# A decode step with gated attention and MLP: the result's cast and write, SP's last wait, and the place of the first load

## The chip, the cores and the metric

The kernel runs on one core of a Trainium2 chip. The core has five engines with instruction queues of their own: TensorE (PE, with its weight loads shown apart as PEld), VectorE (DVE), ScalarE (ACT), GpSimd (POOL) and SyncE (SP, which here only issues DMAs and waits). Sixteen DMA engines move data between the chip's memory (HBM) and the on-chip memory (SBUF); matmuls write to PSUM, in banks of 512 fp32 columns. Engines meet only through semaphores. The metric is the device time of one execution in microseconds.

## The reference

One decode step for four sequences (B = 4) with one new position each. Attention reads the last 4096 positions of a key and value cache with 8 key heads and 32 query heads of 128; an MLP with a ReLU gate runs on the same input; a scalar gate per sequence mixes the two. B_x is not used.

```
g = sigmoid((x * gate_w).sum(-1))              # one number per sequence
q = (x @ wq) -> 32 heads of 128                # x: 4 x 512
p = softmax(q @ k^T / sqrt(128))               # last 4096 of 16384 positions
a = (p @ v) -> 4 x 4096, then @ wo             # 4 x 512
b = ((x @ W_gate) * (x @ W_gate > 0) * (x @ W_up)) @ W_down
out = g * a + (1 - g) * b                      # 4 x 512, bf16
```

All inputs are bf16. The kernel reads 81 MB and writes 4 KB.

## The kernel before

The program is written as a list of operations per engine (class Program, lines 34 to 150). `op` and `dma` append an operation with a name and the names it waits for; `plan` turns these into semaphore values, leaving out waits that an engine has already made; `emit` (line 107) writes an engine's list out. PE's list is written as a loop over pairs of sets; the other engines' lists are straight. All five lists are written out inside one block (lines 562 to 581): at its start each engine jumps to its own code, and at its end each engine drains and all meet in a barrier. A barrier of all engines also stands at the start of the program, under line 595, ahead of the block.

All large loads are issued by SP, in the order in which they are needed (lines 245 to 261): wq (4 MB), then for each of eight sets (a sequence and half of its key heads) K and V of 4 MB each, with two buffers of each, then W_gate, W_up, W_down and wo in four pieces of 2, 1.25, 0.5 and 0.25 MB. A load into a buffer waits for the last reader of what was there. x (4 rows of 1 KB) and gate_w (1 KB) are issued by ACT (lines 243 and 244).

At the start x and gate_w are transposed on PE (line 306), the gate g and 1 - g are made (lines 311 to 319, event G), and q is projected (line 457) when wq has landed. For each set the keys are transposed on PE (line 340) and copied back by ACT and DVE (lines 345, 347), the scores are made (line 373), masked (line 381) and exponentiated (line 410), turned (line 417) and multiplied with V (line 429); `combine` (line 437) adds the parts and writes the attention output, scaled by g and by the softmax sum, into the tile `oq` (line 450). The MLP's hidden values, scaled by 1 - g, go into `hT` (line 483).

Both tiles serve as weights of the last matmuls, with 32 columns for each contraction slice of 128. Only four columns, one for each sequence, hold values, and the rest stay zero. Before the change sequence b stands in column 8b. The last matmuls (lines 545 and 553) are four column tiles side by side: tile c writes rows 32c to 32c + 31 of one bank, with output columns 128c to 128c + 127, so that sequence b's result stands in row 32c + 8b. They accumulate over W_down and then over the pieces of wo as those land.

The end (lines 557 to 559):

```
P.op("dve", lambda e: e.tensor_copy(outs[:, :], AB[:, 0:128]), ("OUTS",), [("ACC",)])
P.dma("sp", ... out.rearrange("b o (c d) -> c (b o) d", d=128), outs[0:128:8, :]), ("OUT",), [("OUTS",)])
P.op("sp", None, None, [("OUT",)])
```

DVE casts the whole bank, 128 rows of 128 columns, to bf16; SP writes every eighth row to its place in the result, sixteen pieces of 256 B; then SP waits for that write, still inside the block, so that the barrier at the block's end comes behind it.

Of the kernel before, what the change touches and what calls it, by code (L numbers as in the profile page):

```python
# [6 lines left out]
BF16 = mybir.dt.bfloat16  # L7
ACTF = mybir.ActivationFunctionType
# [25 lines left out]
class Program:  # L34
# [69 lines left out]
            if name is not None:  # L104
                ins.then_inc(sems[self.events[name][0]], step)

    def emit(self, engine, eng, sems):
        ops, plan = self.ops[engine], self.plan(engine)
        if engine != "pe":
            for op, need in zip(ops, plan):  # L110
                self.put(eng, sems, op, need)
            return
        n = len(self.turns) - 1
        base = []
        for t in range(n + 1):
            level = {}
            for need in plan[:self.turns[t]]:
                level.update({s: v for s, v in need.items() if s in self.lowered})
            base.append(level)
        shift = [{s: base[t + 1].get(s, 0) - base[t].get(s, 0) for s in self.lowered} for t in range(n)]  # L120
        length = self.turns[1] - self.turns[0]
        bodies = []
        for t in range(n):
            assert shift[t] == shift[0] and self.turns[t + 1] - self.turns[t] == length
            body = []
            for k in range(length):
                need = plan[self.turns[t] + k]
                body.append({s: v - base[t].get(s, 0) for s, v in need.items() if s in self.lowered})
                if t > 0:
                    assert all(s in self.lowered for s in need), (t, k, need)  # L130
                    a, b = ops[self.turns[t] + k][1], ops[self.turns[0] + k][1]
                    assert (a is None) == (b is None) and (a is None or self.events[a][0] == self.events[b][0])
            bodies.append(body)
            assert body == bodies[0], [(k, x, y) for k, (x, y) in enumerate(zip(body, bodies[0])) if x != y]
        for k in range(self.turns[0]):
            self.put(eng, sems, ops[k], plan[k])
        for s, v in base[0].items():
            eng.sem_inc(sems[s], -v)
        with eng.Fori(0, n):
            for k in range(length):  # L140
                i = self.turns[0] + k
                need = dict(bodies[0][k])
                need.update({s: v for s, v in plan[i].items() if s not in self.lowered})
                self.put(eng, sems, ops[i], need)
            for s, v in shift[0].items():
                if v:
                    eng.sem_inc(sems[s], -v)
        for i in range(self.turns[n], len(ops)):
            self.put(eng, sems, ops[i], {s: v - base[n].get(s, 0) if s in self.lowered else v
                                         for s, v in plan[i].items()})  # L150


def bass_gated_mix__sliding_block_cached__glu_gated_reglu__decode_kernel(
# [13 lines left out]
    with ExitStack() as ctx:  # L167
        def sb(name, shape, dt):
            return ctx.enter_context(nc.sbuf_tensor(name, shape, dt))
# [33 lines left out]
        recip = sb("recip", [128, 2], FP32)  # L203
        oq = sb("oq", [128, 32, 32], BF16)
        gtmp = sb("gtmp", [128, NFT * 4], FP32)
        gtmp2 = sb("gtmp2", [128, NFT * 4], FP32)
        hT = sb("hT", [128, NFT, 32], BF16)
        outs = sb("outs", [128, 128], BF16)
        banks = [ctx.enter_context(nc.psum_tensor("bank%d" % i, [128, 512], FP32)) for i in range(8)]
        TR = banks[0:NTR]  # L210
        SCB = banks[NTR:NTR + NSC]
# [1 line left out]
        FB = banks[7]  # L213
# [7 lines left out]
        P = Program()  # L221
# [36 lines left out]
        for k in range(len(WO_CUTS) - 1):  # L258
            lo, hi = 512 * WO_CUTS[k], 512 * WO_CUTS[k + 1]
# [14 lines left out]
        for a in range(4):  # L274
            r = slice(32 * a, 32 * a + 32)
# [161 lines left out]
        def combine(s):  # L437
            par, b, half = s % 2, s // 2, s % 2
            r = slice(64 * half, 64 * half + 64)
            for k in range(8):  # L440
                lo = 3 - k % 4 + 64 * (k // 4)
                P.op("pe", lambda e, k=k, lo=lo: e.matmul(FB[r, 256:288], Wsel[:, lo:lo + 64], osb[:, par, 32 * k:32 * k + 32],  # L442
                                                          start=(k == 0), stop=(k == 7)), None,
                     [("OSB", s), ("WSUM",), ("QC", 1), ("G",), ("OQ", s - 1) if s >= 1 else None, ("H",) if s == NSET - 1 else None])
            P.op("pe", lambda e: e.matmul(FB[r, 288:288 + NPIECE], Wsum[:, :], rowsum[:, par, :], start=True, stop=True),
                 ("SUMS", s))
            P.op("dve", lambda e: e.tensor_reduce(ssum[r, par:par + 1], FB[r, 288:288 + NPIECE], AXIS.X, ALU.add),
                 ("SSUM", s), [("SUMS", s)])
            P.op("dve", lambda e: e.reciprocal(recip[r, par:par + 1], ssum[r, par:par + 1]), ("RECIP", s), [("SSUM", s)])
            P.op("dve", lambda e: e.tensor_scalar(oq[r, :, 8 * b], FB[r, 256:288], recip[r, par:par + 1],  # L450
                                                  gsb[r, b:b + 1], op0=ALU.mult, op1=ALU.mult),
                 ("OQ", s), [("RECIP", s), ("G",), ("OQZ",)])

# [18 lines left out]
        def gateup():  # L472
            for i in range(NFT):
                for which, W, key in ((0, Wg, "WG"), (1, Wu, "WU")):
                    col = 64 + 64 * which + 4 * i
                    for t in range(4):
                        P.op("pe", lambda e, W=W, i=i, t=t, col=col: e.matmul(  # L477
                            FB[:, col:col + 4], W[:, t, i:i + NFT * 127 + 1:NFT], xT[:, t * 8:t * 8 + 4],
                            start=(t == 0), stop=(t == 3)),
                            ("GU",) if (i == NFT - 1 and which == 1 and t == 3) else None, [("WG",), ("WU",), ("OQ", NSET - 2)])  # L480
            P.op("dve", lambda e: e.tensor_scalar(gtmp[:, :], FB[:, 64:64 + NFT * 4], 0.0, None, op0=ALU.max), ("H0",), [("GU",)])
            P.op("dve", lambda e: e.tensor_tensor(gtmp2[:, :], FB[:, 128:128 + NFT * 4], gtmp[:, :], ALU.mult), ("H1",), [("H0",)])
            P.op("dve", lambda e: e.tensor_tensor(
                hT[:, :, :].rearrange("p i (b o) -> p i b o", o=8)[:, :, :, 0], gtmp2[:, :].rearrange("p (i b) -> p i b", b=4),
                gsb[:, 4:8].rearrange("p (o b) -> p o b", o=1).to_broadcast([128, NFT, 4]), ALU.mult), ("H",),
                [("H1",), ("G",), ("HZ",)])

# [9 lines left out]
        for s in range(1, NSET):  # L497
# [13 lines left out]
            if s >= 2:  # L511
                combine(s - 2)
# [20 lines left out]
        for k in range(NPIECE):  # L533
            exponent(NSET - 1, k)
        combine(NSET - 2)
        for k in range(NPIECE):
            turn(NSET - 1, k)
        gateup()
        for k in range(4):
            values(NSET - 1, k)  # L540
        combine(NSET - 1)
        AB = SCB[0]
        for i in range(NFT):
# [5 lines left out]
        for k in range(len(WO_CUTS) - 1):  # L549
            for i in range(WO_CUTS[k], WO_CUTS[k + 1]):  # L550
                for cb in range(4):
# [2 lines left out]
                        AB[32 * cb:32 * cb + 32, 0:128], oq[:, i, :], Wo3[:, i, cb * 128:(cb + 1) * 128],  # L554
                        start=False, stop=(i == 31), tile_position=(0, 32 * cb)),
                        ("ACC",) if last else None, [("WO", k), ("OQ", NSET - 1)])
        P.op("dve", lambda e: e.tensor_copy(outs[:, :], AB[:, 0:128]), ("OUTS",), [("ACC",)])
        P.dma("sp", lambda e: e.dma_start(out.rearrange("b o (c d) -> c (b o) d", d=128), outs[0:128:8, :]), ("OUT",), [("OUTS",)])
        P.op("sp", None, None, [("OUT",)])

        sems = {name: ctx.enter_context(nc.semaphore(name)) for name in P.sems}
        with nc.Block() as block:
            @block.sync
            def _(e):
                P.emit("sp", e, sems)

            @block.gpsimd
            def _(e):
                P.emit("pool", e, sems)

            @block.tensor
            def _(e):
                P.emit("pe", e, sems)

            @block.vector
            def _(e):
                P.emit("dve", e, sems)

            @block.scalar
            def _(e):  # L580
                P.emit("act", e, sems)


# [26 lines left out]
```

## Time and profile before

| | |
|---|---|
| time, median of 3 runs | 197.55 us (197.55 to 197.69) |
| the profiled execution's own time | 197.38 us |
| its span, first to last instruction | 195.7 us |
| share of the span: PE, DVE, ACT | 72%, 53%, 47% |
| DMA: bytes, mean rate over the span | 81.19 MB, 415 GB/s |
| last piece of wo awaited until | 192.7 us |
| cast of the result | 193.19, 0.29 us |
| issue of the result's DMA | 193.51, 0.69 us |

A page of the profile shows one execution. A row in order of time gives the start in us, the length in us, engine, line and operation, and tile written "<-" tile read. "SPq" is SP's queue, "ACTq" ACT's. A row of groups gives the number of instructions, the busy time and the mean ns of one, and the idle time ahead of them with what ended it. A row of waits reads "who <- whom: us in total, times, longest us". A row of a window gives its limits and length, the busy time of PE, PEld, DVE, ACT and POOL with the number of instructions, and at the end PE's granted clock, the DMA engines' share and GB/s. In rows with three numbers between slashes these are the least, median and greatest duration in ns.

### The profile page before, as it was taken

Reading aid. Unit: us, or ns where it says so; the run is one execution under the profiler, and the core shown is the slowest. Engines: PE = TensorE matmul, PEld = TensorE weight load, DVE = VectorE, ACT = ScalarE, POOL = GpSimd, SP = SyncE. Lnnn points to the kernel's source line nnn. Section 1 sums busy time; section 2 is a strip of 40 time slices with the busy share of each in tenths; the row PEclk is TensorE's granted clock in tenths of the full one; section 3 lists DMA queues with packets and bytes.
Section 4 is the critical chain, followed back from the end, with each engine's and each line's share of the span. In section 5 each row is a group of like instructions: output and inputs, shape, how many; then the busy total and the mean of one; then the engine's idle time right before and its main releaser. Section 6 shows DMA issues by size and latency. Waiting matters only on the chain.

```text
span 195.7 us, 4263 instructions
## 1 busy us (share of the span) xinstructions
PE 140.6 (72%) x1858; PEld 107.7 (55%) x1858; DVE 103.6 (53%) x278; ACT 91.5 (47%) x108; POOL 7.9 (4%) x39
## 2 busy tenths in 40 slices
PE   0134199968889919992999399929992999498634
PEld 0034197535567518751976286528752875397533
DVE  2102025888599456945585659456945584741200
ACT  2000058698398409760886098509750976220000
POOL 7400000000000000000000000000000000000000
PEclk9999999999999996997599879996996699965855
DMA  6999999999999999999999999999999999999991
GB/s 215 449 429 452 429 449 442 425 429 437 432 422 429 425 429 429 427 429 425 435 429 435 429 429 430 429 429 429 429 429 429 435 411 425 450 431 415 422 385 59
DMA packets 3498, 81.19 MB, mean 415 GB/s; under 512 B 409, under 2 KB 414, under 8 KB 670
## 3 DMA queue, kind: packets, MB, share of 16 engines
q1 hardware_dynamic: 3476, 81.01, 96.8%
q8 instruction: 9, 0.15, 0.3%
q14 instruction: 3, 0.02, 0.0%
q10 hardware_dynamic: 10, 0.01, 0.0%
HBM read 81.01 MB, written 0.00 MB: 414 GB/s over the span
## 4 chain that ended last, share of the span: by engine, by line
DMA 57%; PE 25%; ACT 9%; DVE 4%; issue 1%; SPq 1%
DMA Ksb<-in_A_k_cache_dram 46%; PE bank L340 16%; DMA Wbig<-in_A_wo_dram 12%; ACT Ksb L345 7%; PE bank L373 5%; DVE Ksb L347 2%; PE bank L429 2%; ACT sc L410 2%; PE bank L553 1%; PE bank L442 1%; DVE pT L417 1%; ACT L410 1%; DVE sc L381 1%; SPq L260 0%; DVE oq L450 0%
## 5 line engine op out<-in xcount | busy, mean ns | idle before, releaser
L345 ACT ACTIVATE Ksb<-bank 128x1024 bf16<-128x1024 bf16 x72 | 70.9, 1022 | 68.2 <-PE bank L340 68.0
L340 PE MATMUL bank<-identf,Ksb 128*128 128x128 f32 x512 | 81.1, 313 | 29.4 <-DMA Ksb<-in_A_k_cache_dram 24.0
L340 PEld LDWEIGHTS bank<-identf,Ksb 128*128 128x128 f32 x512 | 66.6, 161 | 44.1 <-DMA Ksb<-in_A_k_cache_dram 25.7
L347 DVE COPY Ksb<-bank 128x1024 bf16<-128x1024 bf16 x56 | 38.0, 685 | 41.8 <-PE bank L340 40.8
L381 DVE CUSTOM_DVE_ANT_0 sc<-bank,mask 128x512 bf16<-128x512 f32 x32 | 21.7, 684 | 9.6 <-PE bank L373 9.5
L429 PE MATMUL bank<-Vsb,pT 128*32 128x256 bf16 x512 | 20.8, 291 | 0.9 <-DMA Vsb<-in_A_v_cache_dram 0.9
L373 PE MATMUL bank<-Ksb,QSP 128*32 128x512 bf16 x256 | 19.4, 383 | 2.1 <-DVE Ksb L347 1.6
L410 ACT ACTIVATE sc<-sc,negmax 128x1024 bf16<-128x1024 bf16 x16 | 18.3, 1146 | 4.8 <-DVE negmax L402 4.7
L417 DVE STREAM_TRANSPOSE pT<-sc 128x1024 bf16<-128x1024 bf16 x16 | 19.7, 1237 | 1.3 <-ACT sc L410 1.0
L429 PEld LDWEIGHTS bank<-Vsb,pT 128*32 128x32 bf16 x512 | 13.2, 101 | 7.1 <-issue 3.3
L442 PEld LDWEIGHTS bank<-osb,Wsel 128*64 128x64 f32 x128 | 8.1, 138 | 4.6 <-issue 2.6
L442 PE MATMUL bank<-osb,Wsel 128*64 128x32 f32 x128 | 8.9, 224 | 1.2 <-DVE osb L434 1.2
L373 PEld LDWEIGHTS bank<-Ksb,QSP 128*32 128x32 bf16 x256 | 4.1, 94 | 9.4 <-DVE Ksb L347 4.4
L477 PE MATMUL bank<-xT,Ksb 128*128 128x4 bf16 x112 | 6.9, 199 | 1.8 <-DVE oq L450 1.8
L477 PEld LDWEIGHTS bank<-xT,Ksb 128*128 128x128 bf16 x112 | 6.8, 160 | 1.9 <-issue 1.9
L553 PE MATMUL bank<-Wbig,oq 128*32 128x128 bf16 x128 | 4.2, 311 | 4.1 <-DMA Wbig<-in_A_wo_dram 4.0
L357 POOL COPY QSP<-QS 128x64 bf16<-128x64 bf16 x8 | 1.8, 236 | 118.2 <-PE bank L373 107.4
L457 PE MATMUL bank<-xT,Wbig 128*128 128x4 bf16 x128 | 3.6, 166 | 4.0 <-DMA Wbig<-in_A_wq_dram 4.0
L306 PE MATMUL bank<-ident,xsb 5*128 5x5 bf16 x4 | 0.3, 167 | 7.9 <-DMA xsb<-in_gate_w_dram 7.9
L553 PEld LDWEIGHTS bank<-Wbig,oq 128*32 128x32 bf16 x128 | 3.1, 140 | 5.0 <-DMA Wbig<-in_A_wo_dram 5.0
L457 PEld LDWEIGHTS bank<-xT,Wbig 128*128 128x128 bf16 x128 | 3.5, 104 | 4.0 <-DMA Wbig<-in_A_wq_dram 4.0
L434 DVE COPY osb<-bank 128x256 f32<-128x256 f32 x8 | 3.4, 420 | 3.6 <-PE bank L429 3.6
(55 smaller groups left out, 47.0 us busy)
## 6 DMA issues: line engine op xcount, KB each, us to landing
Ksb<-in_A_k_cache_dram SPq DMA_DIRECT2D x8, 4096.0 KB, 22.9
Vsb<-in_A_v_cache_dram SPq DMA_DIRECT2D x8, 4096.0 KB, 32.0
Wbig<-in_A_wq_dram SPq DMA_DIRECT2D x1, 4096.0 KB, 12.2
Wbig<-in_A_wo_dram SPq DMA_DIRECT2D x1, 2048.0 KB, 20.2
Ksb<-in_B_W_gate_dram SPq DMA_DIRECT2D x1, 1792.0 KB, 17.9
Ksb<-in_B_W_up_dram SPq DMA_DIRECT2D x1, 1792.0 KB, 21.8
Vsb<-in_B_W_down_dram SPq DMA_DIRECT2D x1, 1792.0 KB, 15.6
Wbig<-in_A_wo_dram SPq DMA_DIRECT2D x1, 1280.0 KB, 22.8
```

The source lines that it names most:

```text
L340: P.op("pe", lambda e, bk=bk, cc=cc, c=c, s=s: e.transpose(bk[:, cc * 128:(cc + 1) * 128], kw[:, c * 128:(c + 1) * 128], identf[:, :]), (" ...
L345: P.op("act", lambda e: e.activation(dst, bk[:, :].bitcast(BF16), ACTF.Copy), ("KTC", s, i), [("KT", s, i)])
L347: P.op("dve", lambda e: e.tensor_copy(dst, bk[:, :].bitcast(BF16)), ("KTC", s, i), [("KT", s, i)])
L373: P.op("pe", lambda e, a=a, h=h: e.matmul(bk[32 * a:32 * a + 32, 0:512], QSP[:, s % 2, h, :], k4[:, 16 * bank:16 * bank + 16, 32 * a:32 * ...
L381: P.op("dve", lambda e: e.tensor_tensor_reduce(sc[:, s % 2, bank * 512:(bank + 1) * 512], bk[:, :], mask[:, :], 1.0, LOWEST, ALU.add, ALU.max,
L410: P.op("act", lambda e: e.activation(sc[:, par, k * PW:(k + 1) * PW], sc[:, par, k * PW:(k + 1) * PW], ACTF.Exp, bias=negmax[:, par:par + ...
L417: P.op("dve", lambda e: e.transpose(pT[:, par, k * PW:(k + 1) * PW], sc[:, par, k * PW:(k + 1) * PW]), ("PTT", s, k), [("EXP", s, k), ("PV ...
L429: P.op("pe", lambda e, c=c, g=g, col=col: e.matmul(OB[32 * g:32 * g + 32, 0:256], pT[:, par, col:col + 32], v3[:, 16 * k + c, :], start=(k ...
L442: P.op("pe", lambda e, k=k, lo=lo: e.matmul(FB[r, 256:288], Wsel[:, lo:lo + 64], osb[:, par, 32 * k:32 * k + 32], start=(k == 0), stop=(k ...
L457: P.op("pe", lambda e, h=h, t=t: e.matmul(FB[:, 64 + 4 * h:68 + 4 * h], Wq3[:, t, 128 * h:128 * h + 128], xT[:, t * 8:t * 8 + 4], start=(t ...
L477: P.op("pe", lambda e, W=W, i=i, t=t, col=col: e.matmul(FB[:, col:col + 4], W[:, t, i:i + NFT * 127 + 1:NFT], xT[:, t * 8:t * 8 + 4], star ...
L553: P.op("pe", lambda e, i=i, cb=cb: e.matmul(AB[32 * cb:32 * cb + 32, 0:128], oq[:, i, :], Wo3[:, i, cb * 128:(cb + 1) * 128], start=False, ...
```

## The change

It has four parts.

1. The four live columns of `oq` and `hT` are columns 0 to 3 instead of 0, 8, 16 and 24. So the result stands in rows 32c to 32c + 3 of the bank.
2. The result tile `outs` is 4 rows of 512 columns instead of 128 rows of 128. Four casts of 4 rows by 128 columns fill it, c = 0 and 2 on DVE, 1 and 3 on ACT; each shifts its rows to rows 0 to 3. SP's write waits for both engines and is a plain copy of four rows of 1 KB.
3. SP's last operation, the wait for that write, is written out behind the block, so behind the block's barrier.
4. SP's first operation, the load of wq, is written out ahead of the block, behind the start-up barrier.

```diff
-    def emit(self, engine, eng, sems):
+    def emit(self, engine, eng, sems, lo=0, hi=None):
         ops, plan = self.ops[engine], self.plan(engine)
         if engine != "pe":
-            for op, need in zip(ops, plan):
+            for op, need in list(zip(ops, plan))[lo:hi]:
                 self.put(eng, sems, op, need)
...
-        outs = sb("outs", [128, 128], BF16)
+        outs = sb("outs", [4, 512], BF16)
...
-            P.op("dve", lambda e: e.tensor_scalar(oq[r, :, 8 * b], FB[r, 256:288], recip[r, par:par + 1],
+            P.op("dve", lambda e: e.tensor_scalar(oq[r, :, b], FB[r, 256:288], recip[r, par:par + 1],
...
-                hT[:, :, :].rearrange("p i (b o) -> p i b o", o=8)[:, :, :, 0], gtmp2[:, :].rearrange("p (i b) -> p i b", b=4),
+                hT[:, :, 0:4], gtmp2[:, :].rearrange("p (i b) -> p i b", b=4),
...
-        P.op("dve", lambda e: e.tensor_copy(outs[:, :], AB[:, 0:128]), ("OUTS",), [("ACC",)])
-        P.dma("sp", lambda e: e.dma_start(out.rearrange("b o (c d) -> c (b o) d", d=128), outs[0:128:8, :]), ("OUT",), [("OUTS",)])
+        for c in range(4):
+            to, src = outs[0:4, 128 * c:128 * c + 128], AB[32 * c:32 * c + 4, 0:128]
+            if c % 2 == 0:
+                P.op("dve", lambda e, to=to, src=src: e.tensor_copy(to, src), ("OUTS", c), [("ACC",)])
+            else:
+                P.op("act", lambda e, to=to, src=src: e.activation(to, src, ACTF.Copy), ("OUTS", c), [("ACC",)])
+        P.dma("sp", lambda e: e.dma_start(out.rearrange("b o d -> (b o) d"), outs[:, :]), ("OUT",), [("OUTS", c) for c in range(4)])
         P.op("sp", None, None, [("OUT",)])
...
+        P.emit("sp", nc.sync, sems, 0, 1)
         with nc.Block() as block:
             @block.sync
             def _(e):
-                P.emit("sp", e, sems)
+                P.emit("sp", e, sems, 1, -1)
...
+        P.emit("sp", nc.sync, sems, -1)
```

## The prediction

> **What bounds the kernel now.** I read the page's slices first, then a summed window, then the tail and the head in order of time, and last the waits of SP's queue and the rows of the block's end.
>
> ```profile
> span 195.7 us, 4263 instructions
> PE 140.6 (72%) x1858; PEld 107.7 (55%) x1858; DVE 103.6 (53%) x278; ACT 91.5 (47%) x108; POOL 7.9 (4%) x39
> DMA  6999999999999999999999999999999999999991
> ...
> 1.70:192.70 191.00, 140.17 (x1850) 107.53 (x1850) 102.66 (x275) 91.51 (x108) 6.97 (x32) 0.89 1.00 425
> ```
>
> The last row is the window from 1.7 to 192.7 us: the DMA engines are busy for a share of 1.00, at 425 GB/s. So 191.0 of 195.7 us are one unbroken transfer. Inside it no engine sets the time. Only three things can change the total: when the transfer begins, how long it is, and what lies ahead of it and behind it. The change moves no load's size and no order of loads, so I look at the first 1.8 us and the last 3.0 us.
>
> ```profile
> 0.81 0.39 SPq L245 DMA_DIRECT2D Wbig<-in_A_wq_dram  x1
> 1.26 1.34 SPq L236 DMA_DIRECT2D Ksb<-in_A_k_cache_dram  x2
> ...
> 192.74 0.43 PE bank L553 x8
> 193.17 0.02 issue
> 193.19 0.29 DVE outs L557
> 193.51 0.69 SPq L558 DMA_DIRECT2D out_dram<-outs  x1
> ```
>
> The head and the tail in order of time: start, length, what. The first big load is issued at 0.81. The tail is a chain with nothing beside it: last matmuls, one cast of 0.29, one output DMA with 0.69 of issue.
>
> ```profile
> SPq L562 <- DMA out_dram<-outs: 1.1, 1, 1.1
> SPq L562 <- PEq L562: 0.2, 1, 0.2
> SPq L595 <- PEq L595: 0.7, 1, 0.7
> ...
> L562 SPq COMPARE_BRANCH  x1: 32/32/32, 195.3 to 195.3; - x1
> L562 SPq DRAIN  x1: 13/13/13, 195.4 to 195.4; - x1
> L562 SPq EVENT_SEMAPHORE  x1: 17/17/17, 195.6 to 195.6; - x1
> ```
>
> SP's waits and the block's end (line 562). SP waits 1.1 us after the issue for the output to land, at 193.51 + 0.69 + 1.1 = 195.3. Only then does it branch out of the block, drain and join the barrier of all engines, which is over at 195.6; the span ends at 195.7. So 0.4 us of barrier stand in series behind the landing. The third row is the start-up barrier, before which SP can issue nothing.
>
> **The change part by part.** The profiled execution took 197.38 us, of which 195.7 is the span and 1.7 lies around it; the median of the runs is 197.55. I make the sum as a difference within that execution and add it to the median. The 1.7 outside I leave as it is.
>
> *wq's load ahead of the block.* The start-up barrier lets SP go near 0.74 (the chain shows 0.74 0.07 issue, then the load at 0.81); I read those 0.07 us as the jump into the block. Issued in front of the jump, the load gains at most 0.07 and at least nothing; some step between a barrier and the next instruction remains, so I take -0.03. Queued behind it on SP are the first K loads (1.26) and V load (2.64); they now pay the jump, but wq takes 12.2 us to land, so K and V issued some 0.1 later are covered; without that cover they would cost that 0.1. What an earlier wq can push back is x and gate_w on ACT's queue: x's packets start at 1.75 to 1.81 and 1.99, wq's at 1.83, and gate_w is already caught, as PE waits for it until 7.86. From there to G takes 1.6 us, wq is awaited until 13.08, and behind the query projection there are 5.4 us (18.4 to 23.86) until K arrives. A further 2 to 4 us for x and gate_w costs nothing.
>
> *The layouts of oq and hT.* Eight casts of oq (0.42 each) and one of hT (0.41) change only the stride of what they write. The last oq ends at 184.9 while PE waits for wo until 187.8, and hT at 178.7 while PE waits for V. Hidden; without the cover, a change of a tenth of these would be 0.04. PE reads the same 32 columns of weights, only with the live ones in front.
>
> *One cast becomes four.*
>
> ```profile
> L319 ACT ACTIVATE gsb<-bank 128x4 f32<-128x4 f32 x1 | 0.2, 168 | 0.0
> L345 ACT ACTIVATE Ksb<-bank 128x1024 bf16<-128x1024 bf16 x72 | 70.9, 1022 | 68.2 <-PE bank L340 68.0
> L461 DVE CAST qTb<-bank 128x128 bf16<-128x128 f32 x1 | 0.3, 290 | 7.9 <-PE bank L457 7.9
> ...
> 17.48 0.88 DVE L468 CAST QS<-bank 64x256 bf16<-64x256 f32 x2 [0.49 <-PE bank L464]
> ```
>
> Groups by shape (mean ns behind the bar), and one row in order of time. A DVE cast costs by columns, not rows: 256 columns take 422 ns on 64 rows here and 420 on 128 rows (line 434). So 4 rows of 128 columns cost the full 0.29. Two of them do not overlap when they start on different rows: L468's two casts (rows 0 and 64, as here) take 0.88 = 2 x 0.42 + 0.03. Two casts therefore take 2 x 0.29 + 0.03 = 0.61 in place of 0.29: +0.32. On ACT, 4 columns take 168 ns and 1024 take 1022, so 128 take about 168 + 124 x 0.84 = 270 ns; L318 and L319 start 0.07 apart (9.17, 9.24), hence two casts end by about 0.45 to 0.55. ACT lies beside DVE and does not set the end. SP now waits for two semaphores instead of one; a barrier's semaphore instruction on SP is 17 ns, and with its dispatch I take +0.03 (bounds 0 to 0.08). Together +0.35 (0.25 if the two casts overlap as neighbouring memsets do, 0.42 at most).
>
> *The output DMA.* Before: 16 pieces of 256 B. After: 4 of 1 KB. No row shows a 1 KB store. The nearest is x's load, 4 pieces of 1 KB in the other direction, on ACT's queue:
>
> ```profile
> 0.80 0.56 ACTq L243 DMA_DIRECT2D xsb<-in_A_x_dram  x1
> ...
> GB/s 0 0 0 0 0 0 0 0 0 0 0 26 51 77 51 26 52 52 26 26 0 26 0 0 0 0 0 0 0 0 0 0 0 0 0 0 0 0 0 0
> GB/s 0 0 0 0 0 0 0 0 0 0 68 0 68 69 0 4369 0 2185 4369 0 0 0 2185 2185 2185 68 0 0 2185 0 0 0 2185 0 0 6554 0 2185 0 0
> ```
>
> The two GB/s rows are windows in 40 slices: 194.7 to 195.1 us (the output, 10 ns a slice) and 1.6 to 2.2 (x as the small numbers, 15 ns a slice). The output's first byte moves at 194.81, 1.30 after its issue began, and its data last 0.11. x's first byte moves at 1.75, 0.95 after its issue began, and three of its four pieces within 0.06. The rest, from last byte to SP's release (195.3 - 194.92 = 0.36), I keep. So 1.75 us becomes about 0.95 + 0.04 + 0.36 = 1.35: -0.40. Bounds: nothing gained or even 0.10 lost if time goes by direction and not by pieces; -0.55 by the one-piece gate_w, whose issue is 0.23 where x's is 0.56. I take x's value, since it has the same four pieces.
>
> A rule speaks against this. The Trainium skill's page "DMA: Bandwidth & Descriptors", section on the anatomy of one DMA, puts most of a fixed 2 us into the receipt of the write at the target, whatever the size; the trace has 1.75 us, but only 0.36 of it behind the last byte. By the page the output would gain nothing and the whole change about -0.04; by the rows it is the sum below.
>
> *SP waits behind the block.* The branch, the drain and the barrier (0.4 us) now run while the output is under way, in the 1.1 us that SP waits. Nothing is queued behind that last wait but the end of the program. Left behind the landing is one semaphore instruction (17 to 50 ns): -0.35. Bounds: -0.40, and +0.02 if SP's drain itself waits for its DMA. The drains I can see (POOL 0.32, DVE 0.33, ACT 2.4 us) last as long as their own engine's work, and SP has none, so I take the value near the first bound.
>
> Sum: -0.03 + 0.35 - 0.40 - 0.35 = -0.43. 197.55 - 0.43 = 197.12; call it 197.1.
>
> **The rivals.**
> - *The drain holds SP until the output has landed*, so that the barrier stays in series: -0.03 + 0.35 - 0.40 + 0.02 = -0.06, 197.5. For it: SP's drain before stood at 195.4, behind the landing, so the trace never shows one with a DMA open. Against: it took 13 ns, as if there was nothing to it.
> - *The store takes as long in four pieces as in sixteen*: -0.03 + 0.35 + 0 - 0.35 = -0.03, 197.5. For it: x is a load, on another queue. Against: the store's longest part lies ahead of its first byte, where pieces are made.
> - *ACT's casts need a table load behind their wait*, which ends on the other side. A table load is 1.28; ACT would end at 193.19 + 1.28 + 0.45 = 194.9 instead of DVE's 193.80, +1.1 on the path: 197.12 + 1.1 = 198.2. It decides once ACT ends 0.43 later than DVE. Against: there are only two such loads, at 1.67 and 39.53, both ahead of the wait they could stand behind (ACT's work starts at 9.17 and 40.83), and 72 copies ran beside exponentials without one.
> - *More is gained than the span shows*: the other engines leave the program 0.7 us earlier, and part of the 1.7 us outside the span may begin with them: up to -0.3 more, 196.8. No view shows it.
>
> **How the numbers follow.** 0.2% is 0.40 us, about what a measurement of this kernel can tell from no change. My forecast has a chance of 0.55 and its own range, from the bounds of casts and store, is 196.9 to 197.3, about six tenths of it beyond 0.2% faster, as -0.43 lies just past -0.40. The extra gain has 0.18, all of it faster. Drain 0.10 and store 0.09, both within 0.2%. Table load, or anything else that late, 0.08. Faster: 0.55 x 0.6 + 0.18 = 0.51; slower 0.08; same the rest, 0.41. The range runs from 196.75 to 197.55, which leaves out the slower case and the far ends.
>
> **What the profile after would show.** wq's issue at 0.74 to 0.80. Two DVE casts of 290 ns with 0.03 between them, two ACT casts of about 270 beside them. SP's output issue about 0.35 after where the first cast's end would have let it go, 0.56 or less long instead of 0.69, first byte 0.95 after it began. SP's drain before the landing, and the span's end within 0.1 of it. I am wrong if the output's first byte still comes 1.3 after the issue, if SP's drain lasts to the landing, or if the transfer in the middle is not 191.0 us long.

## The result, and the profile after

The changed kernel takes 196.70 us (median, 196.40 to 196.87) where the kernel before takes 197.61 beside it: a ratio of 0.9951, interval 0.9938 to 0.9964, or about 0.97 us less by the ratio and 0.91 by the medians. The forecast of 197.1 had the sign right and the size at less than half, and 196.70 lies just below the range, which ends at 196.75. The page of the changed kernel begins with its span; the DMA row is the engines' busy share in 40 slices:

```profile
span 195.2 us, 4267 instructions
...
DMA  6999999999999999999999999999999989999992
```

The window from 1.7 to 192.7 us (limits, length, busy time of PE, PEld, DVE, ACT and POOL, PE's clock, DMA share, GB/s):

```profile
1.70:192.70 191.00, 141.48 (x1850) 107.66 (x1850) 102.41 (x275) 91.43 (x108) 6.97 (x32) 0.88 1.00 425
```

The transfer is as it was, a share of 1.00 at 425 GB/s. The difference lies at the end. First the tail and the head in order of time (start, length, what):

```profile
0.80 0.40 SPq L245 DMA_DIRECT2D Wbig<-in_A_wq_dram  x1
...
193.19 0.56 ACT L562 ACTIVATE outs<-bank 4x128 bf16<-4x128 f32 x2 [21.43 <-PE bank L553]
193.19 0.60 DVE L560 CAST outs<-bank 4x128 bf16<-4x128 f32 x2 [7.44 <-PE bank L553]
193.84 0.35 SPq L563 DMA_DIRECT2D out_dram<-outs  x1
```

Then SP's waits, the rows of the block's end (line 568), and SP's separate wait instructions (line 101):

```profile
SPq L101 <- DMA out_dram<-outs: 0.6, 1, 0.6
SPq L568 <- PEq L568: 0.2, 1, 0.2
...
L568 SPq DRAIN  x1: 167/167/167, 194.2 to 194.2; - x1
L568 SPq EVENT_SEMAPHORE  x1: 17/17/17, 194.6 to 194.6; - x1
...
L101 SPq EVENT_SEMAPHORE  x2: 17/17/17, 193.8 to 195.1; - x2
```

The first cast starts at 193.19 in both profiled executions, so the tails can be laid side by side:

| us | before | after |
|---|---|---|
| store's issue starts | 193.51 | 193.84 |
| issue's length | 0.69 | 0.35 |
| issue's start to SP's release | 1.77 | 1.30 |
| barrier over | 195.6 | 194.6 |
| last wait over | 195.3 | 195.1 |
| end of the span | 195.7 | 195.2 |
| the execution's own time | 197.38 | 196.40 |
| time less span | 1.7 | 1.2 |

The span lost 0.5 us, near the 0.43 of the forecast. The same amount again went from the time around the span, which the forecast left alone. Other executions show it too: the time less the span is 1.67 to 1.86 us in 63 executions of the kernel before and 1.20 to 1.39 in ten of the changed one (spans are recorded to 0.1). That is the question for the experiments.

### The profile page after: what moved, and what is told of

It is laid out like the page before. It is cut to its first block, busy times and chain, and to the rows that moved or that the text cites. A ratio compares the mean times of both kernels' runs of the same rounds, so it can differ in the third digit from the quotient of the medians.

```text
span 195.2 us, 4267 instructions
## 1 busy us (share of the span) xinstructions
PE 141.9 (73%) x1858; PEld 107.8 (55%) x1858; DVE 103.7 (53%) x279; ACT 92.0 (47%) x110; POOL 7.9 (4%) x39
## 4 chain that ended last, share of the span: by engine, by line
DMA 58%; PE 25%; ACT 10%; DVE 4%; issue 1%; SPq 1%; DVEq 0%
DMA Ksb<-in_A_k_cache_dram 46%; PE bank L340 16%; DMA Wbig<-in_A_wo_dram 12%; ACT Ksb L345 7%; PE bank L373 5%; DVE Ksb L347 2%; PE bank L429 2%; ACT sc L410 2%; PE bank L553 1%; PE bank L442 1%; DVE pT L417 1%; ACT L410 1%; DVE sc L381 1%; SPq L260 0%; DVE oq L450 0%
## 5 line engine op out<-in xcount | busy, mean ns | idle before, releaser
L340 PEld LDWEIGHTS bank<-identf,Ksb 128*128 128x128 f32 x512 | 65.3, 159 | 44.3 <-DMA Ksb<-in_A_k_cache_dram 25.9
L442 PEld LDWEIGHTS bank<-osb,Wsel 128*64 128x64 f32 x128 | 8.8, 148 | 4.7 <-issue 2.7
L562 ACT ACTIVATE outs<-bank 4x128 bf16<-4x128 f32 x2 | 0.5, 269 | 21.5 <-PE bank L553 21.4
L442 PE MATMUL bank<-osb,Wsel 128*64 128x32 f32 x128 | 9.7, 233 | 1.2 <-DVE osb L434 1.2
```

The costliest lines, as they stand in the source:

```text
L340: P.op("pe", lambda e, bk=bk, cc=cc, c=c, s=s: e.transpose(bk[:, cc * 128:(cc + 1) * 128], kw[:, c * 128:(c + 1) * 128], identf[:, :]), (" ...
```

## The experiments

One measure is used throughout: in the profiled execution, the own time less the start of the first cast of the result. It leaves out where the long transfer happened to end (193.15 to 193.53 in these executions). It is 197.38 - 193.19 = 4.19 us for the kernel before and 3.21 for the changed one. It agrees between like kernels to about 0.1 (3.21 again in a second profile of the changed kernel). Beside it stands the time less the span, over all executions of a kernel.

### The parts one by one, and the engines held back

Theory A: the four engines that do not wait leave the program while SP still does, and part of the closing work behind the span runs in that time. Theory B: the span's own gain is all there is to the wait, and the rest has another source.

The wait alone, on the kernel before:

```diff
-                P.emit("sp", e, sems)
+                P.emit("sp", e, sems, 0, -1)
...
+        P.emit("sp", nc.sync, sems, -1)
```

> The kernel before with one part of the change: SP's wait for the output stands behind the block; the cast, the store and wq's load are as before. Theory A (the engines that leave early run part of the work outside the span while SP still waits): 0.35 us off the span and 0.45 us off the time around it, so about 0.8 us faster, a ratio near 0.996, with the profiled execution's time less its span near 1.2 in place of 1.7. Theory B, the prediction as written (only the barrier is hidden, the time around the span stays): 0.35 us faster, ratio 0.998, 1.7 around the span.

Measured: 196.89 us, ratio 0.9965 (0.9953 to 0.9977), so 0.69 us less. Own time 196.8, span 195.5: 1.3 around the span, and 1.30 to 1.38 over its six executions. From the first cast (193.38): 3.42, or 0.77 less than before. This is A's number; B's 0.998 lies just outside the interval, and its 1.7 far from the 1.3. SP's wait for the landing and the block's end in this kernel:

```profile
SPq L101 <- DMA out_dram<-outs: 0.4, 1, 0.4
...
L562 SPq DRAIN  x1: 423/423/423, 194.4 to 194.4; - x1
L562 SPq EVENT_SEMAPHORE  x1: 17/17/17, 195.0 to 195.0; - x1
```

SP's drain lasts 0.42 us here and 0.17 in the changed kernel, so the barrier is over only 0.4 us ahead of the landing, not 0.6.

The casts and the store alone:

```diff
-        P.emit("sp", nc.sync, sems, 0, 1)
...
-                P.emit("sp", e, sems, 1, -1)
+                P.emit("sp", e, sems)
...
-        P.emit("sp", nc.sync, sems, -1)
```

> The four casts and the plain store alone: SP's wait and wq's load are inside the block again. Both theories: the casts cost 0.32, the store gains 0.45, together about 0.1 us faster, ratio 0.9993, 1.7 us around the span. If the rest of the gain came from the casts and the store in some way that the trace hides, this kernel would be 0.5 us faster or more.

Measured: 197.47 us, ratio 0.9994 (0.9985 to 1.0004); 197.59 - 195.8 = 1.8 around the span, and 1.69 to 1.85 over its eleven executions. From the first cast (193.44): 4.15, where 4.19 was before. As expected, and not told apart from no change.

The changed kernel without wq's load ahead of the block:

```diff
-        P.emit("sp", nc.sync, sems, 0, 1)
...
-                P.emit("sp", e, sems, 1, -1)
+                P.emit("sp", e, sems, 0, -1)
```

> The changed kernel with wq's load back inside the block. The trace shows its issue 0.007 us earlier by the change, so the same time as the changed kernel within 0.05 us, ratio 0.995 against the kernel before. The rival, that starting the load ahead of the block is worth 0.3 us or more (an unbroken transfer that starts or runs otherwise), gives 0.9965 or more.

Measured: 196.62 us, ratio 0.9952 (0.9938 to 0.9965). This part gives nothing that can be measured. The load is issued at 0.804 us here too, from inside the block, so the 0.007 us by which it came earlier than in the kernel before are not the doing of this part.

All engines held until the output has landed:

```diff
         P.emit("sp", nc.sync, sems, -1)
+        for eng in (nc.scalar, nc.vector, nc.gpsimd, nc.tensor):
+            eng.wait_ge(sems[P.events[("OUT",)][0]], 16)
```

> The changed kernel in which ACT, DVE, POOL and PE too wait for the output behind the block, so that no engine leaves the program before the output has landed; the barrier is still hidden. Theory A: the gain inside the span stays and the one around it goes, 1.7 us around the span again, about 197.1 us, ratio 0.9975. Theory B, or any cause that has nothing to do with the engines' leaving: as the changed kernel, 196.7, ratio 0.995.

Measured: 197.11 us, ratio 0.9981 (0.9972 to 0.9990). Around the span 196.90 - 195.2 = 1.7, and 1.70 to 1.86 over its eleven executions; from the first cast (193.15) 3.75. The four added waits in the trace:

```profile
L591 ACTq EVENT_SEMAPHORE  x1: 17/17/17, 195.1 to 195.1; - x1
L591 POOLq EVENT_SEMAPHORE  x1: 17/17/17, 195.1 to 195.1; - x1
L591 DVEq EVENT_SEMAPHORE  x1: 21/21/21, 195.1 to 195.1; - x1
L591 PEldq EVENT_SEMAPHORE  x1: 51/51/51, 195.1 to 195.1; - x1
```

They end with SP's own wait, and the span is the changed kernel's, 195.2. Yet the time around the span is 1.7 again. Nothing else differs between the two kernels, so theory A holds: it is the early leaving of the other engines that takes 0.45 us off. B falls.

### Which engine waits

If the closing work goes engine by engine, it matters who is last. Each of four kernels gives the last wait to another engine:

```diff
-        P.emit("sp", nc.sync, sems, -1)
+        nc.tensor.wait_ge(sems[P.events[("OUT",)][0]], 16)
```

with nc.scalar, nc.vector and nc.gpsimd in the others.

> The changed kernel with the last wait behind the block made by PE instead of SP. Theory A1: the engines close the program one after another in a fixed order, and SP stands late in it, so that the others' part is done when SP is released; an engine that stands first in that order holds everything, 0.45 us more, about 197.1 us, 1.7 around the span; one in the middle lies between. Theory A2: it only matters that four of five engines are gone, whichever waits: 196.65, 1.2 to 1.3 around the span.

> As the run with PE, with ACT as the engine that waits behind the block. A1: between 196.65 and 197.1, by ACT's place in the order. A2: 196.65.

> As the run with PE, with DVE as the engine that waits behind the block. A1: between 196.65 and 197.1, by DVE's place in the order. A2: 196.65.

> As the run with PE, with POOL as the engine that waits behind the block. A1: between 196.65 and 197.1, by POOL's place in the order. A2: 196.65.

| waits behind the block | median us | ratio (interval) | from the first cast | time less span, all executions | landing to the round's end |
|---|---|---|---|---|---|
| SP (changed kernel, run again) | 196.55 | 0.9949 (0.9932 to 0.9965) | 3.21 | 1.22 to 1.37 | 0.31 |
| DVE | 196.78 | 0.9962 (0.9950 to 0.9975) | 3.34 | 1.35 to 1.46 | 0.44 |
| ACT | 196.84 | 0.9966 (0.9953 to 0.9978) | 3.37 | 1.44 to 1.52 | 0.49 |
| PE | 196.90 | 0.9968 (0.9955 to 0.9980) | 3.52 | 1.51 to 1.64 | 0.63 |
| POOL | 197.15 | 0.9978 (0.9969 to 0.9988) | 3.77 | 1.75 to 1.89 | 0.87 |
| all five | 197.11 | 0.9981 (0.9972 to 0.9990) | 3.75 | 1.70 to 1.86 | 0.87 |

The last column is explained below. By the ratios only POOL and all five stand apart from SP, as the other intervals overlap with SP's; the two last columns put them in one order, with POOL and all five level.

A2, that the waiting engine does not matter, falls: POOL's wait costs 0.56 us against SP's by the time from the first cast, and POOL alone costs all that five together cost. A1 has the order, but not as it was put: the costliest is POOL and not the engine that is first. The trace also holds the updates of semaphores behind the last instruction. One that no line of this kernel uses (number 2) is updated eighteen times there, in two rounds of nine. These are the times in us of the first round, and the update that the waiting engine holds up stands in brackets:

```
before     195.90  195.93  196.15  196.19  196.21  196.31  196.35  196.38  196.43
SP waits   194.86  194.89  195.10  195.15 [195.28] 195.32  195.36  195.39  195.44
PE waits  [195.49] 195.53  195.57  195.61  195.63  195.73  195.77  195.80  195.85
ACT waits  195.14 [195.56] 195.60  195.65  195.67  195.77  195.81  195.84  195.89
POOL waits 195.21  195.24 [196.06] 196.10  196.12  196.22  196.26  196.29  196.34
DVE waits  194.89  194.92  195.13 [195.35] 195.37  195.47  195.51  195.54  195.59
all wait   195.35  195.38  195.66  195.70  195.72  195.82  195.86  195.89  195.94
```

So the round goes PE, ACT, POOL, DVE, SP and back, in steps of 0.02 to 0.05 us, and about 0.1 at the turn where SP was let go earlier. The second round starts 0.79 us behind the first (0.88 in the run with sixteen pieces below), and from the ninth update to the end of the execution there are 0.95 to 1.06 us in every kernel here. So the end of the first round sets the end of the execution. Counted from the landing (the last update of the store's own semaphore), this end comes after 1.17 us before, after 0.31 in the changed kernel, and as in the table's last column in the others.

The Trainium skill's page "Runtime: NRT & Kernel Launch", section on the preamble and postamble breakdown, describes such a round over the five engines, eight hops of 44 ns, for the barrier ahead of a kernel, and names another barrier behind it, without its steps; it gives no order and no engine that is slow to arrive. The round where PE waits agrees with it, 0.36 us from first to last update. The trace adds both: POOL gets to its step 0.54 to 0.57 us after it is let go (195.57 to 196.15 before, 195.51 to 196.06 where POOL waits), SP 0.12 after it (195.16 to 195.28), PE 0.20 to 0.24. In the changed kernel the first four steps are done at 195.15, just before SP is let go at 195.16, and SP stands last. Before, the round came behind the barrier, and POOL's arrival was waited for in series: from 195.6 to the fifth step 0.6 us, against 0.12 now. The difference, 0.48, is what left the time around the span. What POOL does in those 0.5 us no record shows, and this stays open.

### The store: pieces, and who issues it

The changed kernel's four rows, written as sixteen pieces (the tile's rows are padded to keep them apart):

```diff
-        outs = sb("outs", [4, 512], BF16)
+        outs = sb("outs", [4, 4, 136], BF16)
...
-        P.dma("sp", lambda e: e.dma_start(out.rearrange("b o d -> (b o) d"), outs[:, :]), ...
+        P.dma("sp", lambda e: e.dma_start(out.rearrange("b o (c d) -> (b o) c d", d=128), outs[:, :, 0:128]), ...
```

> The changed kernel as it is, beside the next two on the same chip: 196.65, ratio 0.995.

> The changed kernel, whose store writes the same four rows as sixteen pieces of 256 B (the tile's rows are padded so that the pieces cannot join). If the store's time goes by its pieces: issue 0.69 in place of 0.35, first byte 1.3 us after the issue began in place of 0.9, landing 0.40 to 0.45 later, about 197.05 us. If it was the four rows or partitions of the source that made it faster: as the changed kernel, 196.65.

Measured: the changed kernel 196.55, this one 197.34 us, ratio 0.9990 (0.9980 to 0.9999). Its span is 196.2. The issue, and SP's drain behind it:

```profile
194.19 0.83 SPq L563 DMA_DIRECT2D out_dram<-outs  x1
...
L568 SPq DRAIN  x1: 423/423/423, 195.1 to 195.1; - x1
```

The windows of DMA traffic in 40 slices, this kernel from 194.2 to 196.2 us (50 ns a slice), then the changed kernel from 194.6 to 195.0 (10 ns):

```profile
GB/s 0 0 0 0 0 0 0 0 0 0 0 0 0 0 0 0 0 0 0 0 0 0 0 0 0 0 0 0 15 26 21 21 0 0 0 0 0 0 0 0
```

```profile
GB/s 0 102 0 0 0 103 0 0 0 103 0 0 0 103 0 0 0 0 0 0 0 0 0 0 0 0 0 0 0 0 0 0 0 0 0 0 0 0 0 0
```

The first byte moves at about 195.6, 1.4 us after the issue began; in the changed kernel at 194.62, 0.78 after 193.84. From issue to release the sixteen pieces take 1.97 us, the four 1.30. The bytes, the rows and the direction are the same, so the way in which the store is cut makes the time: 0.65 of the 0.67 us lies ahead of the first byte. With the number of pieces the form of the list changes too (four rows of four pieces in place of four rows), and no run separates the two. The penalty is larger than the 0.40 to 0.45 expected, and the time 0.3 us above the 197.05: this store takes its sixteen pieces from four rows with 0.83 of issue, the kernel before took them from sixteen rows with 0.69.

Two stores from two queues, each waiting for one engine:

```diff
-            if c % 2 == 0:
+            if c < 2:
...
+        o2 = out.rearrange("b o d -> (b o) d")
+        P.dma("sp", lambda e: e.dma_start(o2[:, 0:256], outs[:, 0:256]), ("OUT", 0), [("OUTS", 1)])
+        P.dma("act", lambda e: e.dma_start(o2[:, 256:512], outs[:, 256:512]), ("OUT", 1), [("OUTS", 3)])
+        P.op("sp", None, None, [("OUT", 0), ("OUT", 1)])
```

> The changed kernel with two stores of four rows of 512 B: SP writes DVE's half as soon as DVE is done, ACT writes its own half from its own queue. SP's wait for a second engine goes (0.06 us between ACT's release and the issue now). If ACT's store takes no longer than SP's, 0.03 to 0.05 us faster than the changed kernel; if it takes the 0.56 us of issue that x's load took on ACT, 0.1 to 0.2 us slower.

Measured: 196.64 us, ratio 0.9956 (0.9940 to 0.9973), from the first cast 3.23: the changed kernel's time. The two issues:

```profile
193.91 0.27 ACTq L565 DMA_DIRECT2D out_dram<-outs  x1
193.93 0.35 SPq L564 DMA_DIRECT2D out_dram<-outs  x1
```

SP's issue starts 0.03 sooner after DVE's end, as expected, and its store lands 0.07 later after its issue (1.35 for 1.28). ACT's own half lands 1.19 after its issue. Hence the last run, in which ACT issues the whole store:

```diff
-        P.dma("sp", lambda e: e.dma_start(out.rearrange("b o d -> (b o) d"), outs[:, :]), ...
+        P.dma("act", lambda e: e.dma_start(out.rearrange("b o d -> (b o) d"), outs[:, :]), ...
```

> The changed kernel with the store issued by ACT, behind its own casts, in place of SP; SP only waits for it behind the block. In the run with two stores ACT's issue took 0.27 us and its half landed 1.19 us after the issue began, where SP's whole store takes 0.35 and 1.28. If that is ACT's queue, the landing comes 0.09 us earlier and the time is 196.5 to 196.6, at the edge of what the runs can tell; if it was the half size or the second store in flight, nothing changes and the time is as the changed kernel's, 196.55 to 196.7.

Measured: 196.47 us, ratio 0.9946 (0.9933 to 0.9960). The issue is 0.27 long, but the landing comes 1.26 after its start, where SP's takes 1.28. So it was not ACT's queue that made its half quicker; whether it was the half size or being the first of two stays open. From the first cast 3.18 against 3.21. Neither kernel can be told from the changed one, and none found here beats it beyond its interval.

## Why the prediction was wrong

It was wrong at one step: "The 1.7 outside I leave as it is." The time less the span was taken as a constant, a term of nothing, without a row that showed it; it went from 1.7 to 1.2 us. The run with all engines held shows that this belongs to the moved wait, since it gives 1.7 and 197.11 us, almost the forecast. The mechanism had been put down as a rival (more is gained than the span shows), at up to -0.3 and with a chance of 0.18; it was worth 0.45 to 0.5. It was not seen that the four engines' leaving, and POOL's above all, was in series with SP. None of the three signs of being wrong that the prediction names came up, as all three lie inside the span.

The terms inside the span:

- *wq ahead of the block*, -0.03: the issue came at 0.804 in place of 0.811, but at 0.804 without this part too, and that run is no slower. No gain: the 0.07 us ahead of the load was not the jump into the block.
- *Four casts and the second wait*, +0.35: the store's issue starts 0.33 later. DVE's pair is 0.60 and ACT's 0.56, against 0.61 and 0.45 to 0.55. Right in its size; ACT's pair is longer than taken because its second cast starts only after the first one's end (193.48 after 193.45), which costs nothing beside DVE's 0.60.
- *The store*, -0.40: 1.77 became 1.30, -0.47. Its parts were off: the first byte came after 0.78 and not 0.95, and the four pieces start 0.04 apart and take 0.16 in all, not 0.04. That the cut into pieces makes the time is shown by the run with sixteen. The fixed cost of the Trainium skill's page "DMA: Bandwidth & Descriptors", section on the anatomy of one DMA, would have left nothing of this gain, and does not hold for this store: 4 KB took 1.30, 1.77 and 1.97 us in three shapes. The page gives that cost for DMAs issued by GpSimd, and this store is issued by SP, which the prediction did not say. (Its sum by the page is -0.03, as in the rival, and not -0.04.)
- *The barrier behind the landing*, -0.35: 0.38 became 0.02, -0.36. The drain did not wait for the landing, so that rival falls; but the drain is not the 13 ns that the trace of before shows either. It lasts 0.17 us behind a store of four pieces and 0.42 behind one of sixteen, and hides only because the landing is later still.
- *The table load* did not come: ACT's two casts start with DVE's, at 193.19.

Their sum is -0.01 + 0.33 - 0.47 - 0.36 = -0.51 for a forecast of -0.43, and the span's end moved by 0.5. With 0.48 outside, 0.99, against 0.98 between the two own times (197.38 - 196.40).

The parts taken alone gave 0.69 for the wait and 0.12 for casts and store, 0.81 of the 0.97, each with an interval of about 0.24 on either side. 0.10 of the missing 0.16 is in the trace. With the wait moved alone, the store of sixteen pieces and the longer drain end the barrier later, and POOL's step comes at 195.56, after SP has been let go at 195.47; the round then ends 0.41 us after the landing, where the changed kernel's ends after 0.31. The rest is within the intervals.

## What to carry to other kernels

When an output's landing is the last thing a kernel waits for, put that one wait behind the final barrier and on the engine whose way out is shortest, here SP: the barrier, and what the other engines do on leaving, then run under the landing, here 0.7 us without any other change. When an edit changes who leaves a program when, the time outside the span is a term of the sum with bounds of its own, and not a constant. This small store cost by the way it was cut, most of it ahead of the first byte: four rows of 1 KB beat sixteen pieces of 256 B by 0.47 us, which just paid for the 0.33 us of casts that made it possible.

## What the runs showed of the hardware that was not expected

- Behind the last instruction the engines close in the order PE, ACT, POOL, DVE, SP and back. POOL arrives 0.54 to 0.57 us after it is let go, SP 0.12.
- SP's drain behind an open store lasts 167 ns (four pieces) or 423 ns (sixteen), without waiting for the landing 0.5 us and more later.
- The same 4 KB took 0.83 us of issue on SP as sixteen pieces out of four rows, 0.69 as sixteen pieces out of sixteen rows, 0.35 as four whole rows; four rows issued by ACT took 0.27 without landing sooner after their start (1.26 against 1.28).
